# Starting the MoE three attention steps later, with weight conversion spread over 28 steps and the convolution weights converted after the eighth piece

## The chip, the cores and the metric

The kernel runs on one core of a Trainium2 chip. The metric is the device time of one execution in microseconds. Of the kernel before, three timed runs are known: 552.94, 554.08 and 556.78 us, so the median is 554.08 us. A separate execution was recorded by the profiler; all rows of the trace below come from that one.

## The reference

Attention with rotary position encoding, followed by a gated feed-forward block ("MoE" in the code, although there is one expert).

- Attention: 4 batches, 8 heads, 576 tokens, 64 channels per head, in float32. Queries and keys are rotated, `softmax(q k^T / 8)` is taken with its row maximum subtracted, and the result is multiplied by `v`.
- The heads are put side by side, so each batch gives `x` of 576 x 512.
- Feed-forward: `h = relu(x @ w_in)` with `w_in` 512 x 1024; a convolution over three neighbouring tokens, channel by channel, with weights `conv_w` (3 x 1024); `gate = sigmoid(conv)`; `out = (h * gate) @ w_out` with `w_out` 1024 x 512.

The feed-forward weights arrive as 64-bit floats, which the kernel turns into float32 on the chip.

## The kernel before

**Attention steps.** Two heads form a pair; there are 16 pairs, 4 to a batch. Each pair is worked in five steps, 80 steps in all: step 5p+s handles query rows 128s to 128s+127 of pair p (in s=4 the last 64 rows of both heads). The units that the schedule places are:

- S (`emit_S`, lines 199 to 254): the score matmuls, then the row maxima on VectorE (`reds`, line 214) and the exponentials on ScalarE (`exps`, line 218).
- T (`emit_T`, line 256): transposes of the exponentials on TensorE, copied out of PSUM by ScalarE (line 162); the copies for the last 64 keys are the units Trem (line 269). TQ (line 168) transposes the rotated q and k of the next pair.
- E (`emit_E`, line 310): the product with `v`, 20 matmul instructions for one half of the tokens; E0 in the pair's fifth step, E1 in the first step of the next pair. `norm` (line 326) multiplies by the reciprocal sums on VectorE, three and more steps later.

**Two layouts of PSUM.** Before step `WIDE` two score tiles of three banks each and two transpose tiles are held, scores are issued one step ahead (rank 0.5 of the step before), and all PSUM copies go to ScalarE. From step `WIDE` on there are two score tiles of two banks (one per head), two transpose tiles and two tiles for the MoE; scores are issued in their own step and, for a full step, take both score tiles, so the next step's scores need the exponentials of this step to be done.

**Weight conversion** (`conv_w_piece`, lines 484 to 508). Sixteen pieces of 128 x 512, each in three units: `first` (line 443 on ScalarE, into a staging tile "wt"), `mid` (lines 446, 452 and 455 on VectorE), `third` (line 460 on VectorE; it also issues the load of the piece three further on, and defers by two ticks the split on ScalarE, line 503, and GpSimd, line 504). The list `wsteps` (lines 534 to 537) runs `first` of the next piece ahead of `mid` of this one, 48 units in all, and lines 595 to 597 spread them evenly over steps 0 to WIDE-2, at rank 0.4, behind the maxima and exponentials of the step. The tag "wt" has two buffers. `conv_cw` (line 515) converts the convolution weights by the same four operations, one straight after the other, on 32 x 128 elements and with a "wt" buffer; `turn_cw` (line 522) transposes them on TensorE, through one of the two transpose tiles, and copies them out on VectorE.

**MoE.** Six blocks of 288 tokens run beside attention, the block starting at step WIDE + 10 x block; two more follow as a tail. In a block that starts at step n0, eight M1 units (`emit_M1`, line 312: 12 matmuls at line 347, then relu on ScalarE, line 355) stand in steps n0+1 to n0+8. Behind each M1, by counts of TensorE units (2, 5, 7, 9 ticks, shorter near the end), follow the convolution on VectorE (lines 359 and 361), tanh, gate and split. M2 units (`emit_M2`, line 415; six matmuls at line 425 each) of the block before stand four in step n0 (eight where the block opens the third batch) and the rest at n0+1.5, n0+3.5, n0+5.5 and n0+7.5. Step n0+9 holds no MoE unit.

**Order.** Every engine runs its instructions in the order that `emit` writes, sorted by step and rank.

Of the kernel before, what the change touches and what calls it, by code (L numbers as in the profile page):

```python
# [20 lines left out]
def attention_moe_kernel(ctx, tc, q, k, v, w_in, conv_w, w_out, tab, out):  # L21
# [138 lines left out]
    def evac(eng, out, in_, sc=None):  # L160
        if eng == "A" or "m" not in psum:
            nc.scalar.activation(out=out, in_=in_, func=AF.Copy, scale=1.0 if sc is None else sc)  # L162
        elif sc is None:
            nc.vector.tensor_copy(out, in_)
        else:
            nc.vector.tensor_scalar(out=out, in0=in_, scalar1=sc, scalar2=None, op0=ALU.mult)

    def emit_TQ(p, part):
# [5 lines left out]
        if part == "r":  # L174
# [3 lines left out]
            evac("A", KT[p][:, 0:64], ps[:, 64:128])  # L178
            if p * STEPS < WIDE:
                for h in range(2):  # L180
# [75 lines left out]
    def emit_T(p, s, h=None):  # L256
        if p not in PT:
            PT[p] = ptp.tile([128, 9, S], F32, tag="pt", name="pt")
        pt = PT[p]
        ps = t_tile()  # L260
        st = STR[p] if s == 4 else ST[p, s][:, h, 64 * h:64 * h + 512]
        for t in range(4):
            nc.tensor.transpose(ps[:, 128 * t:128 * t + 128], st[:, 128 * t:128 * t + 128], idf)  # L263
        if s == 4:
            evac("A", pt[:, 0:8, 512:S], ps.rearrange("p (k c) -> p k c", k=8))
        else:
            evac("A", pt[:, h:8:2, 128 * s:128 * s + 128], ps.rearrange("p (k c) -> p k c", k=4))
# [169 lines left out]
    def to_f32(pool, w64, w, n):  # L437
        w32 = w64.bitcast(I32).rearrange("p (n t) -> p n t", t=2)
        h, l = w32[:, :, 1], w32[:, :, 0]
        t = pool.tile([128, n], I32, tag="wt", name="wt")[0:w64.shape[0]]  # L440

        def first():
            nc.scalar.activation(out=t.bitcast(F32), in_=h.bitcast(F32), func=AF.Abs)  # L443

        def clamp():
            nc.vector.tensor_scalar(
                out=t.bitcast(F32), in0=t.bitcast(F32), scalar1=bits(F32_TINY), scalar2=bits(F32_HUGE),
                op0=ALU.max, op1=ALU.min,
            )

        def second():
            nc.vector.tensor_scalar(
                out=t, in0=t, scalar1=3, scalar2=0x3FFFFFFF, op0=ALU.logical_shift_left, op1=ALU.bitwise_and
            )
            nc.vector.scalar_tensor_tensor(
                out=t, in0=l, scalar=29, in1=t, op0=ALU.logical_shift_right, op1=ALU.bitwise_or
            )

        def third():
            nc.vector.scalar_tensor_tensor(  # L460
                out=w.bitcast(I32), in0=h, scalar=-(1 << 30), in1=t, op0=ALU.bitwise_and, op1=ALU.bitwise_or
            )

        return first, clamp, second, third
# [19 lines left out]
    def conv_w_piece(i):  # L484
        _, dh, dl, kk, c = WPIECES[i]
        box = {}

        def first():
            box["w"] = late["ws"].tile([128, 512], F32, tag="wf", name="wf")
            box["s"] = to_f32(late["ws"], stage.pop(i), box["w"], 512)  # L490
            box["s"][0]()

        def mid():
            box["s"][1]()
            box["s"][2]()

        def third():
            box["s"][3]()
            load_w(i + 3)
            hi, lo = dh[:, kk, c:c + 512], dl[:, kk, c:c + 512]  # L500

            def split():
                nc.scalar.activation(out=hi, in_=box["w"], func=AF.Copy)
                nc.gpsimd.tensor_tensor(out=lo, in0=box["w"], in1=hi.bitcast(F32), op=ALU.subtract)

            defer(2, split)

        return [first, mid, third]
# [6 lines left out]
    def conv_cw():  # L515
        t = stage.pop("cw")
        w = late["ws"].tile([32, 128], F32, tag="cwf", name="cwf", bufs=1)
        for fn in to_f32(late["ws"], t, w, 128):
            fn()
        stage["cwf"] = w  # L520
# [12 lines left out]
    wcv = [conv_w_piece(i) for i in range(len(WPIECES))]  # L533
    wsteps = [wcv[0][0]]
    for i in range(len(wcv)):
        wsteps += [wcv[i + 1][0]] if i + 1 < len(wcv) else []
        wsteps += wcv[i][1:]

    WIDE = 26
    MB = 10  # L540
    plan = {}
    onpe = (0, 0.5, 1, 2, 4)
# [2 lines left out]
    def at(n, rank, fn):  # L545
        plan.setdefault(n, []).append((rank, len(plan.get(n, [])), fn))

    def emit():
        with tc.manual_schedule(engines=engines):
# [25 lines left out]
            for p in range(NP):  # L575
                n = STEPS * p
                for s in range(STEPS):
                    m = n + s
                    first = m < WIDE
                    if m:  # L580
# [3 lines left out]
                    for h in range(2 if s < 4 else 1):  # L584
                        at(m + 1, 0 if m + 1 < WIDE else 1, lambda p=p, s=s, h=h: emit_T(p, s, h))
                for g, e in ((0, 2), (1, 4), (2, 5)):
# [8 lines left out]
            for i, u in enumerate(wsteps):  # L595
                x = (WIDE - 1) * i // nw
                at(x, 0.4, u)
            at(12, 3, conv_cw)
            at(14, 2, turn_cw)
            moe = {}  # L600
            for blk in range(2 * B - 2):
                n0 = WIDE + MB * blk
                us = [(n0 + 1 + f, lambda blk=blk, f=f: emit_M1(blk, f)) for f in range(NF)]
# [6 lines left out]
            for n in range(max(max(plan), max(moe)) + 1):  # L610
                late["short"] = n >= STEPS * NP - 3
                if n == WIDE:
                    wctx.close()
# [49 lines left out]
            for u in seq + second + m2_units(last) + m2_units(LASTB):  # L663
                u()
                tick()

    emit()


# [41 lines left out]
```

## Time and profile before

| what | value |
|---|---|
| median of three timed runs | 554.08 us (552.94 to 556.78) |
| profiled execution, its own time | 554.89 us |
| span of its trace | 553.1 us |
| TensorE busy | 508.9 us (92% of the span) |
| VectorE busy | 386.5 us (70%) |
| ScalarE busy | 325.1 us (59%) |
| GpSimd busy | 273.2 us (49%) |
| mean granted TensorE clock | 0.99 of full speed |

The span runs from the first to the last instruction; the execution's own time is 1.8 us longer. Busy times of engines overlap, so they don't add up to the span. PE is TensorE's matmul queue, PEld its weight loads, DVE VectorE, ACT ScalarE, POOL GpSimd. In a timeline row the first two numbers are start and duration in us, and a bracket tells how long the engine sat idle before the instruction and what ended that.

### The profile page before, as it was taken

How to read it: one execution, taken by the hardware profiler on the slowest of the kernel's cores; microseconds unless marked ns; L12 is line 12 of the kernel's file. 1: busy time of each engine (PE TensorE's matmuls, PEld its weight loads, DVE VectorE, ACT ScalarE, POOL GpSimd, SP SyncE). 2: the span in 40 equal slices, each digit the busy share in tenths (PEclk: the TensorE clock that was granted, in tenths of full speed). 3: DMA queues.
4: the chain of work that ended last, by engine and by line, in shares of the span. 5: the costliest groups of instructions: out<-in, count | busy, mean ns of one | idle time of the engine just before them, and what ended most of it. 6: DMA issues, size and time to landing. Idle time of an engine off the chain costs nothing.

```text
span 553.1 us, 9298 instructions
## 1 busy us (share of the span) xinstructions
PE 508.9 (92%) x3295; PEld 369.3 (67%) x3295; DVE 386.5 (70%) x624; ACT 325.1 (59%) x870; POOL 273.2 (49%) x341
## 2 busy tenths in 40 slices
PE   2797969788999899999999999999999999999997
PEld 1354444445767477776877677777768677879986
DVE  4878977896588837684768747692677646657961
ACT  2779766877758545675747546663557546324530
POOL 4666857587573817383555637291361203232440
PEclk9999989999999999999999999999999999999999
DMA  7434433423303031030302140210300110000011
GB/s 187 130 101 130 121 104 97 142 75 71 87 1 87 1 83 24 24 84 7 99 2 66 40 106 1 62 45 26 101 0 24 41 42 0 29 33 20 2 38 58
DMA packets 67538, 33.08 MB, mean 60 GB/s; under 512 B 60412, under 2 KB 61220, under 8 KB 67492
## 3 DMA queue, kind: packets, MB, share of 16 engines
q1 hardware_dynamic: 66292, 32.10, 21.0%
q8 instruction: 26, 0.43, 0.3%
q10 hardware_dynamic: 1200, 0.39, 0.3%
q14 instruction: 20, 0.16, 0.1%
HBM read 27.68 MB, written 4.79 MB: 59 GB/s over the span
## 4 chain that ended last, share of the span: by engine, by line
PE 65%; DVE 15%; ACT 14%; issue 3%; DMA 2%; SPq 0%; ACTq 0%; DVEq 0%
PE tp L316 12%; PE sp L206 11%; PE pm L425 10%; PE pm L347 9%; PE tp L263 9%; PE mt L425 6%; ACT st L218 6%; PE mt L347 5%; DVE c L361 5%; ACT pt L162 4%; DVE negm L214 3%; DVE c L359 2%; PE tp L185 1%; DVE xn L328 1%; ACT wt L443 1%
## 5 line engine op out<-in xcount | busy, mean ns | idle before, releaser
L162 ACT ACTIVATE pt<-tp 128x512 f32<-128x512 f32 (+2 forms) x164 | 88.0, 562 | 93.1 <-PE tp L263 91.5
L214 DVE TENSOR_REDUCE negm<-sp 128x1 f32<-128x576 f32 x144 | 102.4, 748 | 39.5 <-PE sp L206 39.2
L379 POOL TENSOR_TENSOR g<-c,g 128x288 fp32r<-128x288 f32 (+4 forms) x88 | 57.0, 659 | 142.9 <-ACT g L378 141.3
L206 PE MATMUL sp<-kT,qT 64*128 64x288 f32 (+4 forms) x556 | 103.9, 470 | 1.2 <-ACT st L218 0.9
L218 ACT ACTIVATE st<-sp,negm 128x576 f32<-128x576 f32 x128 | 93.8, 746 | 15.1 <-DVE negm L214 15.1
L361 DVE SCALAR_TENSOR_TENSOR c<-rr,cw,c 128x288 f32<-128x288 f32 x128 | 96.7, 755 | 4.5
L263 PE MATMUL tp<-tabs,st 128*128 128x128 f32 x512 | 73.9, 285 | 20.3 <-ACT kr L162 7.6
L263 PEld LDWEIGHTS tp<-tabs,st 128*128 128x128 f32 x512 | 56.0, 143 | 46.2 <-issue 14.5
L347 PE MATMUL pm<-xT,winh 128*128 128x290 f32 x384 | 82.8, 308 | 0.5 <-ACT rr L355 0.5
L316 PE MATMUL tp<-pt,vm 128*64 128x290 f32 x512 | 69.6, 414 | 3.7 <-ACT pt L162 3.4
L206 PEld LDWEIGHTS sp<-kT,qT 64*128 64x128 f32 (+1 forms) x556 | 46.6, 177 | 36.0 <-issue 16.7
L425 PE MATMUL pm<-wouth,g 128*128 128x512 f32 x176 | 63.1, 412 | 0.0
L347 PEld LDWEIGHTS pm<-xT,winh 128*128 128x128 f32 x384 | 61.2, 190 | 1.4 <-ACT rr L355 0.7
L347 PE MATMUL pm<-xT,winl 128*128 128x290 f32 x192 | 56.9, 296 | 0.0
L370 DVE SCALAR_TENSOR_TENSOR c<-c,rr 128x288 f32<-128x288 f32 x64 | 39.1, 610 | 20.9 <-ACT c L367 20.2
L316 PEld LDWEIGHTS tp<-pt,vm 128*64 128x64 f32 x512 | 34.0, 136 | 28.8 <-ACT pt L162 5.1
L143 POOL TENSOR_TENSOR t<-rq,tabs 128x512 f32<-128x512 f32 x15 | 20.0, 1334 | 62.7 <-DMA rq<-q 62.1
L367 ACT ACTIVATE c<-c 128x288 f32<-128x288 f32 x64 | 28.3, 443 | 20.8 <-DVE c L361 20.5
L359 DVE TENSOR_SCALAR c<-rr,cw 128x288 f32<-128x288 f32 x64 | 31.2, 488 | 12.0 <-ACT rr L355 11.3
L425 PEld LDWEIGHTS pm<-wouth,g 128*128 128x128 f32 x176 | 33.1, 188 | 9.3 <-issue 2.2
L324 ACT ACTIVATE xn<-tp 128x290 f32<-128x290 f32 x32 | 13.2, 414 | 42.5 <-PE tp L316 42.5
L333 POOL TENSOR_TENSOR xT<-xn,xT 128x290 fp32r<-128x290 f32 x32 | 28.4, 892 | 18.2 <-ACT xT L332 16.9
(97 smaller groups left out, 883.6 us busy)
## 6 DMA issues: line engine op xcount, KB each, us to landing
out<-ot SPq DMA_DIRECT2D x17, 256.0 KB, 2.4
rk<-k SPq DMA_DIRECT2D x32, 128.0 KB, 3.0
w<-moe_w_in SPq DMA_DIRECT2D x8, 512.0 KB
vm<-v SPq DMA_DIRECT2D x32, 128.0 KB, 2.4
w<-moe_w_out SPq DMA_DIRECT2D x8, 512.0 KB, 3.4
rq<-q SPq DMA_DIRECT2D x30, 128.0 KB, 2.5
rb<-rd SPq DMA_DIRECT2D x16, 144.0 KB, 2.9
rb<-rd SPq DMA_DIRECT2D x16, 128.0 KB, 3.0
```

What stands on the lines that cost most here:

```text
L162: nc.scalar.activation(out=out, in_=in_, func=AF.Copy, scale=1.0 if sc is None else sc)
L206: nc.tensor.matmul(out=out, lhsT=qt[64 * h:64 * h + 64, c], rhs=kt[64 * h:64 * h + 64, a:a + n], start=True, stop=True)
L214: reds.setdefault((p, s), []).append(lambda: nc.vector.tensor_reduce(out=nm, in_=sc, axis=AX.XY if len(sc.shape) == 3 else AX.X, op=ALU.ma ...
L218: lambda: nc.scalar.activation(out=dst, in_=sc, func=AF.Exp, bias=nm, scale=1.0, accum_out=sm)
L263: nc.tensor.transpose(ps[:, 128 * t:128 * t + 128], st[:, 128 * t:128 * t + 128], idf)
L316: nc.tensor.matmul(out=xp[64 * h:64 * h + 64, 0:XW], lhsT=vmain[p][:, h, i, :] if i < 4 else vrem[p % 2][:, h, :], rhs=PT[p][:, 2 * i + h ...
L347: nc.tensor.matmul(out=ps[:, 0:XW], lhsT=w[:, kk, fs], rhs=xT[:, xs, e, :], start=(i == 0), stop=(i == n - 1))
L359: nc.vector.tensor_scalar(out=c, in0=r[:, j:j + HS], scalar1=cw[:, f:f + 1], scalar2=None, op0=ALU.mult)
L361: nc.vector.scalar_tensor_tensor(out=c, in0=r[:, j + e:j + e + HS], scalar=cw[:, 8 * e + f:8 * e + f + 1], in1=c, op0=ALU.mult, op1=ALU.add,)
L370: nc.vector.scalar_tensor_tensor(out=c, in0=c, scalar=1.0, in1=r[:, j + 1:j + 1 + HS], op0=ALU.add, op1=ALU.mult)
L379: nc.gpsimd.tensor_tensor(out=lo, in0=c[:, o:o + n], in1=hi.bitcast(F32), op=ALU.subtract)
L425: nc.tensor.matmul(out=ops[tt][:, 0:width], lhsT=g_tile(tt, f, e), rhs=w[:, f, cols], start=(f == 0 and i == 0), stop=(f == NF - 1 and i = ...
```

## The change

`WIDE` goes from 26 to 29. With it the change of PSUM layout, the start of all six blocks, and the last step that holds weight conversion move by three steps. `conv_cw` becomes the 26th of then 49 units of `wsteps`, directly behind `third` of the eighth piece (index 7). Its step is now computed as 28 x 25 / 49, which is 14, at rank 0.4, followed in the same step by `first` of the tenth piece (index 9). `turn_cw` goes from step 14 to step 18.

```diff
     wsteps = [wcv[0][0]]
     for i in range(len(wcv)):
         wsteps += [wcv[i + 1][0]] if i + 1 < len(wcv) else []
-        wsteps += wcv[i][1:]
-
-    WIDE = 26
+        wsteps += wcv[i][1:] + ([lambda: conv_cw()] if i == 7 else [])
+
+    WIDE = 29
...
             for i, u in enumerate(wsteps):
                 x = (WIDE - 1) * i // nw
                 at(x, 0.4, u)
-            at(12, 3, conv_cw)
-            at(14, 2, turn_cw)
+            at(18, 2, turn_cw)
```

## Rows read from the trace of the kernel before

**Rows 1.** The page's first part: busy time of the engines, share of the span, instructions.

```profile
PE 508.9 (92%) x3295; PEld 369.3 (67%) x3295; DVE 386.5 (70%) x624; ACT 325.1 (59%) x870; POOL 273.2 (49%) x341
```

**Rows 2.** Busy time by stretch; each stretch runs from the start of a pair's second E unit (E1, line 316) to the start of the next pair's first (E0): pairs 0 to 1, 1 to 2, 2 to 3, 3 to 4. Columns: stretch, length, busy us of PE, PEld, DVE, ACT, POOL with instruction counts, granted clock, DMA share, GB/s.

```profile
39.39:56.96 17.57, 14.21 (x95) 8.35 (x96) 15.96 (x22) 16.15 (x43) 12.78 (x14) 1.00 0.43 123
61.72:85.65 23.93, 16.95 (x95) 9.61 (x94) 18.02 (x25) 16.83 (x47) 15.15 (x17) 0.86 0.39 113
90.48:108.25 17.77, 14.26 (x94) 8.35 (x93) 14.49 (x18) 15.02 (x41) 10.43 (x9) 1.00 0.51 148
113.07:131.15 18.08, 14.51 (x95) 8.27 (x93) 17.73 (x25) 16.30 (x44) 12.97 (x14) 1.00 0.44 112
```

**Rows 3.** Timeline around `conv_cw` in step 12: its absolute value on ScalarE, the first and the last of its four VectorE operations, the maxima of step 13 behind them, and the transposes of step 13 on TensorE.

```profile
73.65 0.30 ACT L443 ACTIVATE wt<-cw 32x128 f32<-32x128 f32 x1
73.98 1.19 DVE L446 TENSOR_SCALAR wt<-wt 32x128 f32<-32x128 f32 x1 [3.48 <-ACT wt L443]
75.77 1.27 DVE L460 SCALAR_TENSOR_TENSOR cwf<-cw,wt 32x128 int32<-32x128 int32 x1
76.97 1.40 DVE L214 TENSOR_REDUCE negm<-sp 128x1 f32<-128x576 f32 x2
79.29 1.11 PE L263 MATMUL tp<-tabs,st 128*128 128x128 f32 x4 [3.62 <-ACT st L218]
```

**Rows 4.** Busy time by stretch, as in rows 2, of the stretch in which the granted clock was 0.50.

```profile
78.20:85.00 6.80, 5.06 (x16) 2.75 (x16) 4.97 (x8) 5.63 (x13) 3.47 (x5) 0.50 0.23 78
```

**Rows 5.** Timeline of two steps of the kind s=4 (steps 9 and 19) that hold a `first` unit of a weight piece: this unit on ScalarE, the copy of Trem behind it, and the last four matmuls of E0, which read that copy.

```profile
57.11 0.69 ACT L443 ACTIVATE wt<-w 128x512 f32<-128x512 f32 x1
57.69 0.38 ACT L162 ACTIVATE pt<-tp 128x256 f32<-128x256 f32 x1
58.89 0.66 PE L316 MATMUL tp<-pt,vr 128*64 128x290 f32 x4
...
109.28 0.68 ACT L443 ACTIVATE wt<-w 128x512 f32<-128x512 f32 x1
109.86 0.36 ACT L162 ACTIVATE pt<-tp 128x256 f32<-128x256 f32 x1
110.27 0.71 PE L316 MATMUL tp<-pt,vr 128*64 128x290 f32 x4
```

**Rows 6.** Timeline of `turn_cw`'s copy in step 14, and of step 18's two norm multiplies on VectorE with the transposes of step 18's scores that followed on TensorE.

```profile
85.40 0.19 DVE L525 COPY cw<-tp 128x32 f32<-128x32 f32 x1 [2.16 <-PE tp L524]
...
104.87 2.98 DVE L328 TENSOR_TENSOR xn<-xn,rb 128x290 f32<-128x290 f32 x2
106.01 0.66 PE L263 MATMUL tp<-tabs,st 128*128 128x128 f32 x4 [0.55 <-ACT kT L162]
```

**Rows 7.** Busy time by stretch, as in rows 2: from E0 to E1 of pair 4, and from there to E0 of pair 5 (steps 26 to 29, with three M1 units among them).

```profile
131.15:135.41 4.26, 3.68 (x27) 1.96 (x26) 2.94 (x5) 2.33 (x7) 3.91 (x5) 1.00 0.00 0
135.41:155.18 19.77, 18.98 (x134) 14.29 (x134) 11.28 (x17) 14.06 (x38) 12.78 (x23) 1.00 0.25 62
```

**Rows 8.** The chain that ended last, the tail: 144 matmuls of M1 (12 units), then 144 of M2.

```profile
502.45 19.49 PE mt L347 x144
521.94 28.07 PE mt L425 x144
```

**Rows 9.** Busy time by stretch, as in rows 2, each from the start of one step's scores to the start of the next step's: steps 35, 45, 55 and 75, which hold no MoE unit (step 65 has the numbers of 45 and 75), and step 48, which holds one M1 unit and no M2.

```profile
186.00:193.20 7.20, 4.86 (x36) 2.59 (x34) 5.87 (x10) 3.60 (x10) 5.03 (x5) 1.00 0.00 0
248.60:253.71 5.11, 4.64 (x36) 2.67 (x35) 4.30 (x8) 3.21 (x9) 4.84 (x6) 1.00 0.00 0
308.91:314.80 5.89, 4.87 (x37) 2.59 (x35) 5.07 (x9) 3.23 (x8) 4.41 (x5) 1.00 0.00 0
436.39:441.50 5.11, 4.64 (x37) 2.68 (x35) 2.53 (x8) 3.12 (x8) 0.80 (x1) 1.00 0.00 0
...
267.58:271.82 4.24, 4.24 (x33) 3.59 (x32) 4.21 (x6) 2.38 (x6) 4.08 (x4) 1.00 0.44 100
```

**Rows 10.** Timeline of steps 43 and 44: scores of step 43, its maxima, the first of its two exponentials; scores of step 44 and its maxima.

```profile
235.77 1.87 PE L206 MATMUL sp<-kT,qT 64*128 64x288 f32 x8
238.44 1.41 DVE L214 TENSOR_REDUCE negm<-sp 128x1 f32<-128x576 f32 x2
239.57 0.75 ACT L218 ACTIVATE st<-sp,negm 128x576 f32<-128x576 f32 x1
...
242.05 1.19 PE L206 MATMUL sp<-kT,qT 64*64 64x288 f32 x8
245.48 0.75 DVE L214 TENSOR_REDUCE negm<-sp 128x1 f32<-128x576 f32 x1
```

**Rows 11.** Timeline at the seam to the tail: the first M2 unit that needs the last M1 unit of the sixth block.

```profile
489.48 0.50 PE L425 MATMUL mt<-wouth,g 128*128 128x512 f32 x1 [1.16 <-ACT g L378]
```

**Rows 12.** Groups by line: the four VectorE operations of the weight conversion. Columns: count, busy us, mean ns, idle before.

```profile
L460 DVE SCALAR_TENSOR_TENSOR wf<-w,wt 128x512 int32<-128x512 int32 x16 | 17.2, 1074 | 0.7
L455 DVE SCALAR_TENSOR_TENSOR wt<-w,wt 128x512 int32<-128x512 int32 x16 | 16.4, 1026 | 0.6
L452 DVE TENSOR_SCALAR wt<-wt 128x512 int32<-128x512 int32 (+1 forms) x17 | 13.1, 771 | 0.6
L446 DVE TENSOR_SCALAR wt<-wt 128x512 f32<-128x512 f32 (+1 forms) x17 | 12.2, 718 | 3.5 <-ACT wt L443 3.5
```

## The prediction

> **What bounds the kernel now.** I read the page first: TensorE is busy 92% of the span [rows 1], so a change pays by removing TensorE idle time, and costs by adding it. Next I cut the trace into stretches to see where that idle time lies. In the conversion stage, the stretch from E1 of one pair to E0 of the next takes 17.57, 17.77 and 18.08 us, with some 3.5 us of TensorE idle in each; the one from pair 1 to 2 takes 23.93 us [rows 2]. Their mean without the long one is 17.81. VectorE was busy 14.49 us in one of the three and 17.73 in another, and the lengths differ by 0.31: the stage runs at the pace of the loop from scores through maxima, exponentials, transposes and copies, not at VectorE's. Once MoE units stand between the units of attention, TensorE has hardly any idle time: step 48 is 4.24 us long and 4.24 busy; only steps without a MoE unit show gaps [rows 9].
>
> The long stretch has one cause. `conv_cw` in step 12 lets VectorE wait 3.48 us for ScalarE, then run four operations from 73.98 to 77.04; the maxima of step 13 come behind them at 76.97, and TensorE waits 3.62 us for the exponentials [rows 3]. In the same place the granted clock is 0.50, the 1.2 GHz level, for 6.80 us, after TensorE had been idle [rows 4].
>
> **The change part by part.** TensorE's work stays what it is: no unit is added, M1 and M2 units move by three steps. So each term is idle time.
>
> 1. *The stall of step 12 goes*: 23.93 less 17.81, **-6.1 us**. Its other end is -3.6: the stretch at 1.2 GHz had 5.06 us of matmuls, 2.5 us of it owed to the clock, and another gap could bring that back.
>
> 2. *conv_cw at its new place.* In step 14 it stands behind the maxima and exponentials of an s=4 step, and `first` of piece 9 stands right behind it. Of the two "wt" buffers one then belongs to piece 8, whose `mid` comes in step 15; so `first` of piece 9 takes the buffer of `conv_cw` and waits, on ScalarE, until VectorE has finished all four operations. Behind it on ScalarE is the copy of Trem, and E0's last four matmuls wait for that. Worked out on steps 9 and 19 [rows 5]: the absolute value takes 0.30 us, the four operations 3.06 as they ran, or about 1.2 if all go as quickly as the two in the middle (0.60 us together, from 75.17 to 75.77) [rows 3], `first` 0.68 and the copy 0.36. From 109.28 that ends at 111.8 to 113.7, where the matmuls started at 110.27; from 57.11 (0.69 and 0.38 there) at 59.7 to 61.5, against 58.89. So TensorE waits 1.5 to 3.4 us by the one and 0.8 to 2.6 by the other. I take the mean of the four ends: **+2.1**.
>
> 3. *turn_cw in step 18.* Its transpose takes a turn of the two transpose tiles, and its copy stands behind the first of the two norm multiplies: 104.87 plus half of 2.98 plus 0.19 is 106.55, where the next step's transposes began at 106.01 [rows 6]. **+0.55**, between 0 (the copy's wait of 2.16 us in step 14 disappears, and might have cost something outside the long stretch) and 1.2.
>
> 4. *Steps 26 to 28 in the conversion stage.* Before, E0 of pair 4 to E0 of pair 5 took 4.26 and 19.77 us [rows 7] with three M1 units in it; an M1 unit costs TensorE 19.49/12 = 1.62 us [rows 8], so attention took 24.03 - 4.87 = 19.16. Without MoE units the same steps cost 17.81 and, from the gaps between the stretches of rows 2 (4.76, 4.83, 4.82), 4.80: 22.61. **+3.45**. At best 2.3, as pair 6's first scores (1.1 us) now fall behind the stretch; at worst 5.4, if the first scores in the new PSUM layout, which can't be issued ahead, wait as in term 5.
>
> 5. *The step without MoE units.* This is the term that the change hides. Block starts move from step 5k+1 to step 5k+4, so the MoE-free step n0+9 moves from 35, 45, 55, 65, 75 to 38, 48, 58, 68, 78. Before, it held E1, which covers the chain: idle 2.34, 0.47, 1.02, 0.47, 0.47, in sum 4.77 us [rows 9]. Now it is an s=3 step with scores, eight transposes and one TQ, and the next scores can't start before the first exponential is done. Step 43 has the same units in front of it (an M1 and two small units), and its exponentials don't depend on the M1 that follows: scores at 235.77, first exponential over at 240.32 [rows 10], 4.55 us. TensorE's own work there is step 48 less its M1 unit: 4.24 - 1.62 = 2.62. So 1.93 us idle, five times 9.65, less 4.77: **+4.9**. At best -4.8 (nothing waits any more). At worst the maxima come as late as in step 44, 2.24 us after the scores instead of 0.80 [rows 10]: 1.44 more each, +12.1.
>
> 6. *The end.* Between E1 of the last pair and the tail stand seven M1 and four M2 units in place of four and two, with no attention between them; M1 units go to VectorE and ScalarE, and the seam waited 1.16 us for them before [rows 11]. I take half such a wait more, **+0.6**, from -1.2 (it vanishes) to +2.3 (two more).
>
> 7. *Thinner conversion.* VectorE's four operations take 58.9 us [rows 12], now over 28 steps, so 3/28 of it, 6.3 us, leaves the first 25. By the lengths of rows 2 a us of VectorE is worth 0.31/3.24 = 0.1 us there: **-0.6**, between 0 and -6.3.
>
> At nothing: loads of weight pieces keep their distance of three pieces on SP's queue; GpSimd's splits move with their pieces; all copies of steps 26 and 27 that go to ScalarE instead of VectorE are in term 4's price, as the stretches of rows 2 hold them. If the loads came late, a `first` would wait, in the loop of term 2.
>
> Sum: -6.1+2.1+0.55+3.45+4.9+0.6-0.6 = +4.9. On the profiled execution, 554.89, that is 559.8; the median of the runs is 0.81 lower, so **559.0 us**. Under 1% (5.5 us, about what a measurement of this kernel can tell) counts as no change: 548.5 to 559.6.
>
> **Rivals.**
>
> *Faster: VectorE does set the pace of the conversion.* For it: VectorE is busy 17.73 of 18.08 us in one stretch, and its operations vary widely. Then term 7 is -6.3 and the sum -0.8: 553.3. With terms 2, 4 and 5 at 0.8, 2.3 and 0 besides, the sum is -8.2 and the time 545.9. Against it: the 14.49 us stretch, hardly shorter. The Trainium skill, SBUF — State Buffer, section "SBUF: two separate sides", says that VectorE operations with two SBUF inputs and GpSimd operations exclude each other for a whole instruction; by that rule fewer conversion operations per step also means fewer such collisions. The trace agrees in that the same operation takes very different times, but no row shows that its length moved a stretch. Chance 0.24, half of it below 548.5.
>
> *Slower: the free step costs as step 44 suggests.* The mechanism is term 5: the convolution of the block's last M1 stands on VectorE ahead of the maxima of the free step, so scores, maxima and exponentials run bare. Price 12.1 instead of 4.9, giving 566.2. It decides from a lateness of about 0.9 us: above that the sum passes 5.5. For it: step 35, already MoE-free, is 2.34 us idle, E1 notwithstanding. Against it: step 43's 0.80. Chance 0.19.
>
> *The change doesn't remove its stall.* ScalarE instead of VectorE waits, 3.4 us, and the clock falls again for 2.5: terms 1 and 2 are -3.6 and +3.4, the sum +8.7, 562.8. For it: the wait in the order of the "wt" buffers is certain, its length isn't. Against it: step 35's gaps of 2.34 us left the clock at 1.00. Chance 0.09.
>
> **How the numbers follow.** The forecast case, small errors of both signs about its sum, has 0.48; its own range is 554 to 563, its time 559.0, and 0.14 of the 0.48 is put above 559.6. Faster: half of the first rival, 0.12. Slower: 0.14 from the forecast case and 0.28 from the other two rivals, 0.42. No change: the rest, 0.46. For 8 in 10 the range reaches from 549.5, leaving out the deep half of the faster rival, to 566, where the slower one stands.
>
> **What would show it.** The stretch from pair 1 to pair 2 falls from 23.93 to about 20 and has no clock at 0.50 (term 1); a wait on ScalarE for the fourth operation of `conv_cw`, and E0 of pair 2 split before its last four matmuls (term 2); E1 of pair 4 to E0 of pair 5 some 17.8 us long (term 4); steps 38, 48, 58, 68, 78 each about 4.6 us with 2 us idle (term 5); no more than 2 us of waiting before the tail (term 6). The forecast is wrong upwards if those five steps take over 5.5 us, and downwards if the other conversion stretches shrink below 17 us.

## The result, and the profile after

The changed kernel took 562.96 us, the median of four runs (557.95 to 564.44), beside 553.81 us for the kernel before (four runs, 552.94 to 556.78). The ratio is 1.0123, with a 95% interval from 1.0079 to 1.0166 (the quotient of the two medians, 1.0165, is at its upper end): slower, by an amount whose interval reaches to both sides of 1%. Two more comparisons of the same two kernels gave 1.0067 [1.0043, 1.0091] and 1.0124 [1.0086, 1.0163]. The forecast was 559.0 us with a range from 549.5 to 566. The profiled execution of the changed kernel is the fastest of the four, 557.95 us, 3.06 us above the profiled execution before; the forecast sum was +4.9.

The first part of the page answers to [rows 1]. TensorE is busy 2.3 us longer, in a span 3.0 us longer, though no unit was added; some of the waiting is booked as busy, as with the scores of step 48 below.

```profile
PE 511.2 (92%) x3289; PEld 369.0 (66%) x3289; DVE 373.0 (67%) x622; ACT 323.3 (58%) x872; POOL 269.0 (48%) x341
```

Busy time by stretch of the changed kernel, with the columns of [rows 2]. The first, second, fourth and fifth rows are the stretches from E1 of one pair to E0 of the next, the third is E0 to E1 of pair 2, and the last two are those of [rows 7], now without MoE units.

```profile
38.80:55.87 17.07, 14.16 (x93) 8.35 (x92) 12.85 (x20) 15.22 (x42) 7.35 (x8) 1.00 0.48 136
60.70:77.91 17.21, 14.25 (x94) 8.34 (x93) 14.04 (x17) 15.11 (x42) 11.22 (x12) 1.00 0.47 135
77.91:85.86 7.95, 5.04 (x33) 2.44 (x32) 7.02 (x10) 3.61 (x10) 7.71 (x11) 1.00 0.28 78
85.86:104.00 18.14, 14.36 (x95) 8.49 (x94) 15.81 (x21) 15.44 (x42) 9.62 (x10) 1.00 0.39 108
108.83:126.44 17.61, 14.25 (x93) 8.34 (x93) 13.02 (x17) 16.23 (x45) 12.60 (x15) 1.00 0.44 124
126.44:131.27 4.83, 4.83 (x33) 2.55 (x33) 4.66 (x8) 2.52 (x9) 3.83 (x4) 1.00 0.07 13
131.27:147.97 16.70, 13.11 (x87) 7.78 (x86) 13.02 (x17) 14.33 (x40) 13.07 (x15) 1.00 0.29 72
```

The stretch of 23.93 us is gone: 17.21 stands in its place, and the granted clock is 1.00. What follows it is new: E0 to E1 of pair 2, 4.83 us before, takes 7.95, with 2.91 us in which TensorE has no work. The timeline of that place answers to [rows 3 and 5].

```profile
78.33 0.30 ACT L443 ACTIVATE wt<-cw 32x128 f32<-32x128 f32 x1
78.67 0.46 DVE L446 TENSOR_SCALAR wt<-wt 32x128 f32<-32x128 f32 x1 [1.57 <-ACT wt L443]
...
81.20 0.77 DVE L460 SCALAR_TENSOR_TENSOR cwf<-cw,wt 32x128 int32<-32x128 int32 x1
...
82.00 0.66 ACT L443 ACTIVATE wt<-w 128x512 f32<-128x512 f32 x1 [3.37 <-DVE cwf L460]
...
82.57 0.37 ACT L162 ACTIVATE pt<-tp 128x256 f32<-128x256 f32 x1
...
82.99 0.71 PE L316 MATMUL tp<-pt,vr 128*64 128x290 f32 x4 [2.91 <-ACT pt L162]
```

Read from below: the last four matmuls of E0 wait for the copy of Trem; it stands on ScalarE behind `first` of the tenth piece; that waits 3.37 us for the fourth VectorE operation of `conv_cw`, whose buffer it takes. Every wait is where term 2 put it, and E0 is split before its last four matmuls.

The steps without an MoE unit are now 38, 48, 58, 68 and 78. Busy time by stretch, each from a step's scores to the next step's, in this order, as in [rows 9]:

```profile
192.65:197.33 4.68, 3.97 (x25) 2.53 (x23) 3.86 (x8) 3.74 (x13) 2.15 (x2) 1.00 0.57 131
255.13:259.83 4.70, 3.54 (x21) 2.24 (x20) 4.04 (x8) 3.85 (x14) 3.02 (x4) 1.00 0.55 123
317.20:321.90 4.70, 3.54 (x23) 2.26 (x22) 4.06 (x7) 3.76 (x13) 2.21 (x3) 1.00 0.55 124
379.36:384.02 4.66, 3.50 (x23) 2.24 (x22) 4.06 (x8) 3.81 (x14) 3.09 (x4) 1.00 0.55 123
446.47:451.97 5.50, 2.98 (x17) 1.83 (x16) 5.14 (x10) 3.82 (x11) 1.51 (x2) 1.00 0.00 0
```

They take about 4.7 us, and 5.50 in step 78. The idle time shown is 0.71 us in step 38 and 1.16 us in each of the next three; part of the loss hides in the scores, which wait halfway for an exponential: they are booked with 1.89 us in step 48, with 1.17 in step 70. In step 78 the idle time is 2.52 us: there the lags of the MoE are short, and in the timeline ScalarE does tanh (449.12), a transpose copy, the gate's split (449.95) and another copy and split ahead of the first exponential at 451.11.

### The profile page after: what moved, and what is told of

Read it like the earlier page. It is cut to its first block, busy times and chain, and to the rows that moved or that the text cites. A ratio compares the mean times of both kernels' runs of the same rounds, so it can differ in the third digit from the quotient of the medians.

```text
span 556.1 us, 9292 instructions
## 1 busy us (share of the span) xinstructions
PE 511.2 (92%) x3289; PEld 369.0 (66%) x3289; DVE 373.0 (67%) x622; ACT 323.3 (58%) x872; POOL 269.0 (48%) x341
## 4 chain that ended last, share of the span: by engine, by line
PE 77%; ACT 14%; DVE 6%; issue 2%; DMA 1%; ACTq 0%; DVEq 0%
PE sp L206 14%; PE tp L316 14%; PE pm L347 13%; PE pm L425 12%; PE tp L263 10%; PE mt L425 6%; ACT st L218 5%; PE mt L347 5%; ACT pt L162 4%; PE tp L185 1%; DVE c L361 1%; DVE negm L214 1%; PE tp L275 1%; ACT wt L443 1%; PE tp L280 1%
## 5 line engine op out<-in xcount | busy, mean ns | idle before, releaser
L162 ACT ACTIVATE pt<-tp 128x512 f32<-128x512 f32 (+2 forms) x165 | 89.3, 561 | 83.3 <-PE tp L263 80.6
L206 PE MATMUL sp<-kT,qT 64*128 64x288 f32 (+4 forms) x544 | 105.2, 475 | 7.0 <-ACT st L218 7.0
L263 PE MATMUL tp<-tabs,st 128*128 128x128 f32 x512 | 72.3, 281 | 17.4 <-ACT kr L162 7.1
L361 DVE SCALAR_TENSOR_TENSOR c<-rr,cw,c 128x288 f32<-128x288 f32 x128 | 84.6, 661 | 4.5
L347 PEld LDWEIGHTS pm<-xT,winl 128*128 128x128 f32 x192 | 36.6, 191 | 0.0
L359 DVE TENSOR_SCALAR c<-rr,cw 128x288 f32<-128x288 f32 x64 | 27.8, 434 | 12.3 <-ACT rr L355 12.1
L425 PE MATMUL pm<-woutl,g 128*128 128x512 f32 x88 | 34.8, 395 | 0.0
```

What stands on the lines that cost most here:

```text
L206: nc.tensor.matmul(out=out, lhsT=qt[64 * h:64 * h + 64, c], rhs=kt[64 * h:64 * h + 64, a:a + n], start=True, stop=True)
L347: nc.tensor.matmul(out=ps[:, 0:XW], lhsT=w[:, kk, fs], rhs=xT[:, xs, e, :], start=(i == 0), stop=(i == n - 1))
L361: nc.vector.scalar_tensor_tensor(out=c, in0=r[:, j + e:j + e + HS], scalar=cw[:, 8 * e + f:8 * e + f + 1], in1=c, op0=ALU.mult, op1=ALU.add,)
L425: nc.tensor.matmul(out=ops[tt][:, 0:width], lhsT=g_tile(tt, f, e), rhs=w[:, f, cols], start=(f == 0 and i == 0), stop=(f == NF - 1 and i = ...
```

## The experiments

**1. Where the runs of the changed kernel differ.** The changed kernel was run twice more.

> The changed kernel once more, to see where the 5 us lie that most of its runs take beyond its first profiled one (557.95 against 561.5 to 564.4). Theory (clock): TensorE is granted 1.2 GHz in one more place, right behind the step with the longest TensorE gap that the change made, step 15 with 2.91 us; a profile of a run at 562 to 564 shows a stretch of about 13 us at 0.50 from about 83 us on and the same idle time as before, and a profile of a run at 558 shows none. Rival 1: the second stretch at 0.50 lies elsewhere, behind step 28 (idle 2.31 us, at 145 us) or step 78 (2.52 us, at 452 us). Rival 2: no further stretch at 0.50; the steps themselves are longer in those runs, by 2 to 3 us in the conversion stage.

> The changed kernel a third time, to see whether the times of 561.5 to 564.4 of its first comparison (granted clock 0.985 to 0.991) come back and where the clock falls then. Theory (clock): what its runs differ by is the number of stretches at 1.2 GHz, each 3.41 us or a multiple long, behind steps with over 2 us of TensorE idle time (3, 15, 28, 78); the lengths of the steps at 2.4 GHz are the same as in the two earlier profiles, so a run at clock 0.997 takes 558 to 560 and one at 0.985 takes 562 to 564. Rival: runs of equal granted clock differ by 3 us or more, so something else than the clock sets them apart.

Measured: 559.66 us (8 runs; before 556.16) and 561.31 us (6 runs; before 554.93). Of all 18 runs, the seven at a mean granted clock of 0.997 took 557.95 to 559.85 us, three at 0.994 took 559.57 to 560.88, five at 0.991 took 561.20 to 561.78, one at 0.988 took 563.28 and two at 0.985 took 564.41 and 564.44. Runs of one clock differ by at most 1.9 us, so the second expectation's rival falls. The place is seen by laying three profiles side by side: of each, the stretch behind step 15 (step 16) and the one behind step 78 (step 79 up to E0). First the profile of the execution of 557.95 us, then 559.29, then 561.42.

```profile
84.12:89.62 5.50, 5.49 (x39) 2.96 (x37) 4.89 (x6) 3.30 (x10) 4.13 (x4) 1.00 0.00 0
451.97:457.12 5.15, 5.15 (x31) 3.66 (x31) 1.87 (x3) 3.14 (x8) 1.96 (x3) 1.00 0.00 0
```

```profile
83.34:88.84 5.50, 5.49 (x39) 2.96 (x38) 4.90 (x6) 3.31 (x10) 4.12 (x4) 1.00 0.00 0
451.71:458.44 6.73, 6.73 (x30) 4.96 (x30) 1.88 (x3) 3.15 (x8) 1.95 (x3) 0.75 0.01 2
```

```profile
84.47:91.57 7.10, 7.08 (x39) 3.34 (x38) 4.90 (x6) 3.43 (x10) 4.12 (x4) 0.76 0.15 47
454.06:460.60 6.54, 6.54 (x31) 4.32 (x31) 1.87 (x3) 3.15 (x8) 1.96 (x3) 0.78 0.00 0
```

The idle time in front is the same each time, 2.91 and 2.52 us. Behind it the clock stays at 1.00, or falls to 1.2 GHz: 0.76 over 7.10 us is 3.4 us at half speed. A fall costs 1.4 to 1.6 us, with TensorE busy throughout. Both places occur, so theory and rival 1 of the first expectation are each half right; the single stretch of about 13 us that the theory expected does not occur. The two falls in the last profile make 1.60 + 1.39 of the 3.47 us by which it is longer than the first.

There is a third place, in step 3, and it was in the trace of the kernel before already. First the transposes there with the gap ahead of them, then the stretch at 0.50, with the columns of [rows 2]:

```profile
27.10 1.97 PE L263 MATMUL tp<-tabs,st 128*128 128x128 f32 x8 [2.22 <-ACT kr L162]
27.00:30.40 3.40, 3.30 (x12) 2.09 (x14) 1.32 (x3) 2.33 (x7) 1.60 (x2) 0.50 0.82 213
```

In the changed kernel's profiles the gap there is 1.76, 2.13 and 1.94 us; a fall of 3.4 us follows the first and the third and none the second. So the profile of 557.95 us, the fastest, holds one fall too, and the three profiles hold one, one and three, in the order of their clocks 0.997, 0.997 and 0.991. An estimate for the others: (1 - 0.997) x 2 x 558 is 3.3 us at half speed, and (1 - 0.985) x 2 x 562 is 17. The runs at 0.985 were not recorded by the profiler, so where their further falls lay is open; none is seen behind step 28 in the three profiles.

**2. The convolution weights alone, MoE from step 26 as before.**

```diff
-    WIDE = 29
+    WIDE = 26
```

> Of the change only the convolution weights: conv_cw behind the eighth piece and turn_cw in step 18, with the MoE from step 26 as before. Theory (terms 1 to 3 add up, terms 4 to 7 belong to the later MoE): terms 1 to 3 are -6.1, +2.1 and +0.55, so 3 to 6 us less than the kernel before, 548 to 551; with 25 steps for the conversion conv_cw falls in step 12 and the next piece in step 13, so the wait for the buffer should be shorter than 3.37 us and the gain nearer 6. Rival: the stall only changes its place, ScalarE waits instead of VectorE and TensorE with it, and the clock falls again: within 1.5 us of the kernel before, 552 to 555.

Measured: 549.04 us (6 runs; before 556.16), ratio 0.9881 [0.9851, 0.991]. This half of the change makes the kernel faster, by 7.1 us, more than the 3 to 6 expected. In the trace `conv_cw` falls in step 12 and the next piece in step 13; from E0 of pair 0 to E0 of pair 4 it is 92.21 us where the kernel before took 96.66. The two spans differ by 5.4 us, 4.45 of it there and 0.84 ahead of E0 of pair 0, where the kernel before has the fall of step 3 and this one has none. No trace places the other 1.7 of the 7.1; they go with the clock, as its runs were granted 0.993 to 1.000, those of the kernel before beside them 0.984 to 0.994. With a buffer of its own for `conv_cw`:

```diff
-        t = pool.tile([128, n], I32, tag="wt", name="wt")[0:w64.shape[0]]
+        t = pool.tile([128, n], I32, tag=tag, name=tag, bufs=bufs)[0:w64.shape[0]]
...
-        for fn in to_f32(late["ws"], t, w, 128):
+        for fn in to_f32(late["ws"], t, w, 128, "cwt", 1):
```

> As the run before (convolution weights at the new place, MoE from step 26), with a staging buffer of its own for conv_cw. Theory: no wait of ScalarE is left and the stall of 6.1 us goes whole: 547 to 548.5, the fastest of all. Rival: if the wait for the buffer costs nothing with 25 steps, the same as without the buffer, within 1 us.

Measured: 550.36 us (6 runs), ratio 0.9898 [0.9867, 0.9928]; E0 to E1 of pair 2 takes 5.68 us with and without. The theory fails, and the rival holds as far as these runs can tell: the medians are 1.3 us apart, a little more than its 1 us, and the ranges overlap (547.89 to 552.49 and 548.00 to 551.84). Where the next piece comes a step later, no wait for the buffer is left to remove: in the trace without the buffer of its own, `first` stands at 75.45, and the fourth operation of `conv_cw` is over at 72.63.

So of the change of +3.5 us beside the same runs of the kernel before, the weights' new place gives -7.1 and the later MoE takes +10.6 (559.66 less 549.04). The two profiles, 8.4 us apart, tell where: with the M1 and M2 units taken out as in the table below, +5.3 lies between E0 of pair 5 and E1 of pair 15, which hold the free steps, +2.1 in steps 26 to 28, and 0.3 to 0.4 each ahead of E0 of pair 0, from there to E0 of pair 4, and at the end. The remaining 2.2 stand in no profile; the granted clock was 0.991 to 0.997 in these runs.

**3. The buffer in the changed kernel.** The same edit with the MoE from step 29.

> The changed kernel with a staging buffer of its own for conv_cw, so that the next weight piece no longer waits on ScalarE for conv_cw's four VectorE operations. Theory (term 2): step 15 loses its 2.91 us of TensorE idle time, at most 0.6 stays: the profiled execution falls from 557.95 to about 555.3. If the clock falls behind that gap, the median falls with it from 563 to 555 or 556. Rival 1: the idle time goes, but the clock falls elsewhere: the median stays at 560 to 561. Rival 2: the copy of Trem is late for another reason (VectorE's queue), the gap stays above 2 us and the time at 561 to 564.

Measured: 560.26 us (8 runs; the changed kernel beside it 559.66), no gain. The gap of step 15 is gone (5.11 us for E0 to E1 of pair 2) but the next stretch is 21.53 us long where it was 18.14, at most 1.7 us of it through the clock (0.92 over the stretch). Its timeline:

```profile
82.45 1.50 DVE L446 TENSOR_SCALAR wt<-wt 128x512 f32<-128x512 f32 x1
83.99 1.38 DVE L452 TENSOR_SCALAR wt<-wt 128x512 int32<-128x512 int32 x1
85.41 1.10 DVE L455 SCALAR_TENSOR_TENSOR wt<-w,wt 128x512 int32<-128x512 int32 x1
...
87.29 1.36 DVE L214 TENSOR_REDUCE negm<-sp 128x1 f32<-128x576 f32 x2
...
88.69 0.74 ACT L218 ACTIVATE st<-sp,negm 128x576 f32<-128x576 f32 x1 [1.53 <-DVE negm L214]
...
91.34 1.93 PE L263 MATMUL tp<-tabs,st 128*128 128x128 f32 x8 [2.84 <-ACT qT L162]
```

VectorE has a queue here: it shows no idle time from 81.12 to 90.50, and the maxima of step 16, whose scores began at 80.33, come at 87.29, behind three conversion operations of which the first two take 1.50 and 1.38 us (0.42 and 0.43 for the next piece, at 90.50 and 90.95). In the changed kernel the same maxima start at 87.10, hardly earlier. TensorE waits 2.84 us in step 17 instead of 2.91 in step 15, and the clock falls behind that. The time is rival 1's, but neither the theory nor a rival had said that the gap itself only moves: the wait for the buffer is real, and VectorE was as late.

**4. conv_cw one piece earlier,** so that it ends step 12 (run with the edit of experiment 5).

```diff
-        wsteps += wcv[i][1:] + ([lambda: conv_cw()] if i == 7 else [])
+        wsteps += wcv[i][1:] + ([lambda: conv_cw()] if i == 6 else [])
```

> The changed kernel with the later M2 units two steps later (552.0) and conv_cw behind the seventh weight piece instead of the eighth: it then ends step 12 and the next piece begins step 13, as with the MoE from step 26, instead of both standing in step 14. Theory (term 2: the idle time of 2.9 us in step 15 comes from the next piece's wait for conv_cw's buffer in the same step): that idle time falls to 1.1 or less, 549.5 to 550.5. Rival (VectorE has to make up the work of conv_cw somewhere, as when the buffer was its own): a gap of 2 us or more opens in steps 12 to 17, the time stays at 551.5 to 553.

Measured: 549.66 us (4 runs; before 555.83), ratio 0.9889 [0.9853, 0.9925], as the theory has it; the interval just meets that of experiment 5, 0.9915 to 0.9973, so the gap below is the surer evidence. The stretches of rows two to four of the profile after, in this kernel:

```profile
61.90:79.89 17.99, 14.39 (x94) 8.35 (x93) 14.65 (x20) 14.55 (x41) 12.26 (x13) 1.00 0.40 114
79.89:85.58 5.69, 5.05 (x33) 2.45 (x33) 5.13 (x10) 4.17 (x11) 3.48 (x4) 1.00 0.50 143
85.58:103.67 18.09, 14.35 (x94) 8.48 (x93) 14.37 (x19) 15.72 (x44) 13.30 (x16) 1.00 0.38 109
```

The three make 41.77 us, against 43.30 in the changed kernel and 43.87 with the buffer alone, and E0 to E1 of pair 2 idles 0.64 us by this row where it idled 2.91. The rival's gap of 2 us or more in steps 12 to 17 isn't there: the longest there is 1.24 us. What counts is that `conv_cw` and the next piece don't share a step.

**5. The step without an MoE unit.** The later M2 units of each block stand two steps later, the last in step n0+9.

```diff
-                    us += [(n0 + (i / ne if i < ne else 1.5 + 8.0 * (i - ne) / (len(m2) - ne)), u) for i, u in enumerate(m2)]
+                    us += [(n0 + (i / ne if i < ne else 3.5 + 8.0 * (i - ne) / (len(m2) - ne)), u) for i, u in enumerate(m2)]
```

> The changed kernel with the later M2 units of each block moved two steps later, so that the last of them stands in the step that has no MoE unit (48, 58, 68 and 78; step 38 stays without one). Nothing else is moved, no unit is added. Theory (term 5: that step pays for its bare chain of scores, maxima and exponentials): steps 48, 58 and 68 lose their 1.16 us of idle time and the stretch of the scores, about 1.9 us each, step 78 its 2.52 us: 6 to 8 us less than the changed kernel, 552 to 554 where the changed kernel takes 559.7. The clock falls of the earlier profiles at 453 us, right behind step 78's gap, should be gone too. Rival: the idle time goes to the steps that the M2 units leave, and the time stays within 2 us of the changed kernel.

Measured: 552.04 us (12 runs; before 556.09), ratio 0.9944 [0.9915, 0.9973]: faster than the kernel before, and 7.6 us below the 559.66. Steps 48, 58, 68 and 78 of this kernel:

```profile
255.52:260.22 4.70, 4.70 (x27) 3.34 (x27) 4.05 (x8) 3.85 (x14) 3.02 (x4) 1.00 0.42 95
315.99:320.68 4.69, 4.69 (x27) 3.34 (x27) 4.05 (x8) 3.75 (x13) 2.97 (x3) 1.00 0.42 96
376.55:381.21 4.66, 4.66 (x27) 3.34 (x26) 4.04 (x8) 3.81 (x14) 3.08 (x4) 1.00 0.46 104
442.08:447.58 5.50, 4.38 (x24) 2.85 (x23) 5.15 (x10) 3.83 (x11) 1.52 (x2) 1.00 0.00 0
```

They are as long as before, with six matmuls more in each: an M2 unit of 1.40 us cost nothing there, though only 1.16 us had shown as idle in steps 48, 58 and 68. The difference isn't in the scores, which are booked with 1.89 us in step 48 of either kernel; the first M2 matmul starts 0.24 us ahead of the booked end of the transposes before it (258.19 against 257.34 plus 1.09). The gain lies in the places that the units left: the stretch from E1 of pair 7 to E0 of pair 8 fell from 22.78 to 21.19, and from E0 of pair 5 to E1 of pair 15, with as many units in both, from 317.01 to 311.16, four times 1.40 and a little. The rival falls. The clock fell behind step 15 in this profile, and not behind step 78, whose idle time is now 1.12 us.

The same shift with the MoE from step 26, where the free step is one that holds E1 and idles 0.47 us:

> Convolution weights at the new place, MoE from step 26, and the later M2 units two steps later, so that the last stands in steps 45, 55, 65 and 75, which hold E1. Theory (E1 covers the chain in those steps; their idle time is 0.47, 1.03, 0.47 and 0.47 us): at most 2 to 3 us less than without the shift, 546.5 to 548.5 where the kernel before takes 556. Rival (what the M2 units leave gets as much idle time): 549 to 550, no gain.

Measured: 549.89 us (6 runs; before 555.83), ratio 0.9903 [0.9878, 0.9929], against 0.9881 without. The rival holds. Step 45 takes 5.96 us where it was 5.11, and idle time appears in steps 58 and 68, right behind steps 57 and 67, which an M2 unit left: 1.03 and 1.19 us. What pays is to fill an idle step, not the shift.

**6. Other starting steps.** With the MoE from step 24 the free step is again an s=3 step, with 25 an s=4 step that holds E0.

```diff
-    WIDE = 29
+    WIDE = 24
```

> The changed kernel with the MoE from step 24: five conversion steps fewer, but the step without MoE units is the same s=3 step (33, 43, 53, 63, 73). Theory (terms 4 and 5 add up): against the run with the MoE from step 26 (549.0) it gains two conversion steps of 1.15 us each and pays the free steps, 4.9: 551 to 552; against the changed kernel it gains five times 1.15 plus what the stage's later steps cost: 553 or less. Rival (the extra time is the number of conversion steps, the free step costs nothing): 546 to 547. Second rival (23 steps are too few for the conversion and VectorE or ScalarE hold up the first MoE units): 556 or more.

> As the run before (MoE from step 24) with the later M2 units two steps later, in the free steps 43, 53, 63 and 73. Theory: the free steps' 4.9 us go and the gain of the shorter conversion stage stays: 546 to 547.5, below the run with the MoE from step 26. Rival (what the M2 units leave behind costs as much): 551 to 552 as without.

> The changed kernel with the MoE from step 25, so that the step without MoE units is an s=4 step (34, 44, ...), which holds E0, twenty matmuls that don't need the scores of the step. Theory (it is the bareness of the s=3 step that costs, not its lack of an MoE unit as such): little idle time in those steps, as with E1 in the kernel before; one conversion step fewer than with 26: 547.5 to 549. Rival (any step without an MoE unit costs 1 us or more): 552 to 554.

Measured: 563.40 us (ratio 1.015 [1.0117, 1.0183]), 555.63 us (0.9999 [0.9977, 1.0021]) and 561.48 us (1.011 [1.0079, 1.014]), where the kernel before took 556.09. All three missed. The 563.40 lies in the range of its second rival, but not for its reason: M1 units are not held up (from E0 of pair 4 to E0 of pair 5 it is 26.63 us with five M1 units in it, 18.5 without, against 19.16 in the kernel before). The shift of M2 is again worth 7.8 us, and with 25 the free steps, which hold E0, idle less: 0.88 us in step 54 and 0.72 in step 64. That agrees with term 5's mechanism. What I had not reckoned with is that a different number of conversion steps puts every piece elsewhere. From 24, step 9:

```profile
61.62 0.67 ACT L443 ACTIVATE wt<-w 128x512 f32<-128x512 f32 x1 [3.29 <-DMA w<-moe_w_in]
62.19 0.58 ACT L162 ACTIVATE kT<-tp 128x512 f32<-128x512 f32 x1
...
62.82 0.48 PE L263 MATMUL tp<-tabs,st 128*128 128x128 f32 x1 [4.51 <-ACT kT L162]
```

The load of a weight piece is late, `first` holds ScalarE for it, and TensorE stands still for 4.51 us, after 3.44 us at 24.48. At these gaps the clock falls to 0.50, for 6.8 and 10.2 us. From 25, step 13:

```profile
75.46 0.30 ACT L443 ACTIVATE wt<-cw 32x128 f32<-32x128 f32 x1
...
75.79 0.21 DVE L446 TENSOR_SCALAR wt<-wt 32x128 f32<-32x128 f32 x1 [2.86 <-ACT wt L443]
...
78.28 0.47 PE L263 MATMUL tp<-tabs,st 128*128 128x128 f32 x1 [3.07 <-ACT kr L162]
```

This is term 2's wait in another step. `conv_cw` and the next piece share step 12, the next piece waits 1.15 us for the four operations (76.91) and takes 0.66, and behind it stand copies that TensorE needs at once. With the MoE from step 26, where the two don't share a step, TensorE waits 1.24 us in the same place; 3.07 less 1.15 and 0.66 is 1.26. Here, too, the clock falls for 6.8 us at the gap, and once more for 6.8 us at 131. So it is the step into which a unit falls that decides, not its place in the list.

**7. The spreading of the conversion alone.**

```diff
-                x = (WIDE - 1) * i // nw
+                x = 25 * i // nw
```

> The changed kernel with the weight conversion spread over 25 steps as before instead of 28, the MoE still from step 29. It tells what the spreading alone is worth. Theory (term 7: a small gain; scores, maxima, exponentials and copies set the pace): from E0 of pair 0 to E0 of pair 4 as long as with the MoE from step 26 (92.2 us; the changed kernel takes 92.5), steps 26 to 28 a little shorter for want of conversion work: within 2 us of the changed kernel, 558 to 561. Rival (VectorE sets the pace of the conversion, the deep half of rival A): the stretch from E0 of pair 0 to E0 of pair 4 is 3 us longer or more than in the changed kernel and the time 562 or more.

Measured: 559.40 us (6 runs; before 555.83), ratio 1.0075 [1.0045, 1.0105], against 1.0067 for the changed kernel. From E0 of pair 0 to E0 of pair 4 it is 92.21 us against 92.47 in the changed kernel. In sum the spreading is worth nothing: outside the stretch from E0 to E1 of pair 2 the thinner conversion saves 2.0 us (84.52 against 86.50), and in that stretch the stall of step 15 takes 2.2 back (7.95 against 5.71). The shorter steps 26 to 28 that were expected don't show (21.55 against 21.53 us). Behind step 78 this profile holds a fall of 6.8 us, twice as long as those of experiment 1: from step 79's scores to E0 of pair 15 it is 7.94 us where 5.15 was the length at 1.00.

## Why the prediction was right or wrong

By its own terms, on the two profiled executions (M1 units at 1.62 us and M2 units at 1.40 taken out of stretches that hold more of them):

| term | forecast | measured | from |
|---|---|---|---|
| 1, stall goes | -6.1 | -6.72 | 23.93 to 17.21 |
| 2, conv_cw's new place | +2.1 | +3.12 | 4.83 to 7.95 |
| 3 and 7, turn_cw, thinner conversion | -0.05 | -1.11 | the time to E1 of pair 1, 61.72 to 60.70, and from E1 of pair 2 to E0 of pair 4, 40.67 to 40.58 |
| 4, steps 26 to 28 | +3.45 | +2.37 | 19.16 to 21.53 |
| 5, the free step | +4.9 | +4.99 | E0 of pair 5 to E1 of pair 15, 314.82 to 317.01, two M2 units fewer |
| 6, the end | +0.6 | +0.35 | E1 of pair 15 to the last instruction |

The rows sum to +3.0, as the spans differ; the forecast sum was +4.9.

*Right: terms 1 and 5.* The stall left as it was priced, and the clock with it. The free step, the term that the change hides, came to 0.1 us of its price. That it came so close is in part luck: the row is the balance of the whole stretch, and the steps differ (4.7 us long and 0.71 or 1.16 us of visible idle time in place of 4.55 and 1.93, and 5.50 and 2.52 in step 78 for the short lags, which I had not looked at). That TensorE has room in these steps is shown by experiment 5: a unit of work put there costs nothing.

*Term 2* had the mechanism and the upper part of its range: the four operations took 3.30 us from first start to last end (78.67 to 81.97), as slow as before, and not the mean that I took. Experiment 3 adds what it missed: VectorE is as late as the buffer.

*Terms 3 and 7.* Term 3's wait is there, and longer than its price: TensorE waits for the copy of `turn_cw` in step 18, where [rows 6] had 0.55 us.

```profile
101.35 1.06 PE L263 MATMUL tp<-tabs,st 128*128 128x128 f32 x8 [1.52 <-DVE cw L525]
```

That is about +1.0, so some -2.1 of the -1.11 is left for term 7 (0.52 of it ahead of E0 of pair 0), and experiment 7 gives the thinner conversion -2.0 by another way: the term had the right sign and was priced at -0.6. The two errors hid each other.

*Term 4* came out at its lower end, as the stretch without MoE units took 16.70 us, not 17.8.

*The rivals.* The deep half of the first rival ("rival A" in experiment 7), VectorE as the pace of the whole stage, falls: the thinner conversion saved 2 us, not 6.3. The rule of the Trainium skill cited there (SBUF — State Buffer, section "SBUF: two separate sides") is not contradicted: the conversion's four operations of [rows 12] cost 3.3 us less in sum (58.9 to 55.6) when spread thinner; whether for fewer such collisions, no run separates. VectorE does set the pace in single places, as experiment 3 shows.

*Wrong: the clock.* The sum holds no clock term beside term 1's. The step that failed is in the third rival, "Against it: step 35's gaps of 2.34 us left the clock at 1.00", and the chance of 0.09 drawn from it. From that one row I took a gap of two to three us to be safe. In the trace of the kernel before, a gap of 2.22 us in step 3 was followed by 3.4 us at 0.50, which the prediction leaves out. In the changed kernel the clock falls in some executions behind the 2.91 us of step 15 and the 2.52 of step 78, and even behind 1.76 us in step 3. The sum fits the executions with little of it (557.95 to 559.85 at 0.997, the forecast 559.0), and there, too, it is 1.9 us above the profile; that the forecast lies so near to the medians, 562.96, 559.66 and 561.31, is luck in part, a sum too high and falls left out. The median of the first comparison, 562.96, lies beside that rival's 562.8, though not by its price: a fall of 3.4 us costs 1.4 to 1.6 us here and not 2.5, and the runs differ in how many they have. "Slower" should have had more than the 0.42 it got.

*What would show it,* item by item: the stretch from pair 1 to 2 fell further than to 20 (17.21), since the stall of term 2 stands behind E0 and not in it; no clock at 0.50 there in the first profile, but in a later one behind it; the wait on ScalarE and the split E0 as described; E1 of pair 4 to E0 of pair 5 16.70 and not 17.8; the five steps about 4.7 us with 0.7 to 1.2 us idle, so under the 5.5 that would have meant the slower rival, but for step 78, which is at it.

Both kernels are beaten by two versions, and they end level: the weights' new place with the MoE from step 26 (0.9881), and the changed kernel with the later M2 units and with `conv_cw` one piece earlier (0.9889).

## What to carry to other kernels

When the start of an interleaved stage is moved, look for the step that gets no filler and ask which chain lies bare in it; if there is one, move a unit of the filler into it before judging the move. A list of units spread by division over a number of steps is a new schedule for every number: price it by which units share a step and who waits in that step's queues, not by its mean density. And a gap on TensorE has a second price, a chance of a slow stretch behind it, which one profile of either kind cannot show.

## What the runs showed of the hardware

The same gap leaves the clock alone in one execution and is followed by 1.2 GHz in another: step 15's 2.91 us was followed by 1.00 in two profiles and by a fall in a third. Nor does the longer gap alone decide: 1.76 us in step 3 was followed by a fall, 2.13 us there in another execution was not. The falls of the changed kernel's profiles lasted 3.4 us and cost 1.4 to 1.6 us in stretches in which TensorE was busy all the time. The one of 6.8 us in experiment 7 cost 2.8; the kernel before had one of 6.80 [rows 4], and with the MoE from step 24 one lasted 10.2.

VectorE's operations on 32 x 128 elements, the four of `conv_cw`, took 0.21, 0.21, 0.28 and 0.28 us with the MoE from step 25, and 0.46, 1.19, 0.78 and 0.77 in the changed kernel.
